# Chunk attention feeding a bilinear feed-forward: values of one unit and scores of the next in one run on the 64x64 tiles

## The chip, the cores and the metric

The kernel runs on one core of one Trainium2 chip. TensorE (PE) does the matrix products, VectorE (DVE), ScalarE (ACT) and GpSimd (POOL) the elementwise work, and SyncE (SP) issues the transfers. The metric is the device time of one execution in microseconds (us): 309.52 us is the median of three runs of the kernel before (309.21 to 310.18).

## The reference

Attention is local: a sequence of 576 positions is cut into chunks of 64, and each chunk attends to itself alone. Its result, 4608 tokens by 512 features, goes through a bilinear feed-forward layer.

```python
B, H, S, D = 8, 8, 576, 64           # chunks of 64 along S
scores = q_c @ k_c.T / sqrt(D)       # 64x64 for each chunk and head
attn = exp(scores - max)
attn = attn / (sum(attn) + 1e-9)
x = (attn @ v_c) as (B*S, H*D)       # 4608 x 512
out = ((x @ w_a) * (x @ w_b)) @ w_out  # d_ff = 1536
```

All inputs and the output are float32; the kernel computes in bfloat16 and float16 with float32 sums.

## The kernel before

**Tiling.** The 4608 tokens are nine blocks K of 512 tokens, each of two units U of 256. A unit's attention is four steps: `scores(U)` (L244) makes 32 matmuls of 64x64 and two Exp activations on ACT (L260); `sums(U)` (L262) makes four matmuls of 64x512 with ones and two Ln activations (L277); `inverse(U)` is one Exp on ACT (L286); `values(U)` (L290) makes 32 matmuls of 64x64 and two multiplications on DVE that leave `xT` in float16 (L309). The 64x64 matmuls use the array as four quarter tiles; all others use the whole 128x128.

**The feed-forward layer.** From block 2 on, both layers are computed by a seven-product (Strassen-like) scheme on 2x2 blocks. A `Group(K, i)` (L394, i = 0 to 5, 256 columns of the inner dimension) makes the seven products p1 to p7 of the first layer, each of four matmuls of 128x256 (L412). Its sums live in three PSUM banks: A (`pa`), B (one of two `pb` banks in turn) and C (`pc`). ACT copies between products: A into B after p1 (L430), and u, b, v out to SBUF after p6, p2, p5 (L423). `add7` adds v and u on DVE (L450, L451; L451 rewrites C), and after p3 and p4 DVE multiplies B and C into `ab` (L462, twice). p3 and p4 of a group come in the next group's time. `OutGroup(K)` (L498) makes the second layer of the block before in 14 parts (n, th), n = 0 to 6, each of six matmuls (L548). n = 0 and 1 go to A (bank `po`), n = 2, 3 and 5 to B (bank `pq`), n = 4 and 6 to C (`po` again). After (0, 1) ACT copies A into B (L560), after (1, 1) A out (L563), after (2, 1) B out as `uo_sb` (L568), after (3, 1) B out as `vo_sb` (L571), after (5, 1) B out (L575).

**Order.** The order on each engine is the order in which the program issues the work (`manual_schedule`). A group's time has two halves. Written as (i, half) of block K:

| | PE order in half 0 | PE order in half 1 |
|---|---|---|
| group i | p1; parts; p3 of the group before; attention; p6; p4 of the group before | p2; parts; attention; p5; p7 |

How many parts of the second layer are issued in each half is in `chunks` (L802); what attention step is issued is in `attention` (L776 to L799), where U = 2K + 2, the first unit of the next block. In blocks 3 and later: sums U at (0, 0), inverse U at (1, 0), values U at (1, 1), scores U+1 at (2, 1), sums U+1 at (3, 0), inverse at (3, 1), values U+1 at (4, 1), `combine_x` for the next block at (5, 0) (two DVE additions, L392), scores U+2 at (5, 1). Block 2 issues scores U itself at (0, 0) and sums U at (0, 1). There is no attention work left in block 8.

**Banks and loads.** PSUM has eight banks: `pa`, `pc`, `po`, `pq` one each, `pb` and `pt` two each. From the end of block 1 every attention step takes its two banks from `pt` (`spread`, L767). Loads, casts (POOL, L207) and DMA transposes (SP, L234) of a unit are issued by `bring` at (1, 0) and (3, 0), some groups ahead of their use.

Of the kernel before, what the change touches and what calls it, by code (L numbers as in the profile page):

```python
# [16 lines left out]
def kernel(  # L17
# [14 lines left out]
    PSUM = bass.MemoryType.PSUM  # L32
# [9 lines left out]
    NKT = DM // 128  # L42
# [3 lines left out]
    NBLK = NTOK // BLK  # L46
    NU = NTOK // UNIT
    WCOL = 256
    NWP = DFF // WCOL
# [12 lines left out]
    c_pool = ctx.enter_context(tc.tile_pool(name="csb", bufs=1))  # L62
    o_pool = ctx.enter_context(tc.tile_pool(name="osb", bufs=2))
    psum_a = ctx.enter_context(tc.tile_pool(name="psuma", bufs=1, space=PSUM))
    psum_b = ctx.enter_context(tc.tile_pool(name="psumb", bufs=2, space=PSUM))
    psum_c = ctx.enter_context(tc.tile_pool(name="psumc", bufs=1, space=PSUM))
    psum_o = ctx.enter_context(tc.tile_pool(name="psumo", bufs=1, space=PSUM))
    psum_q = ctx.enter_context(tc.tile_pool(name="psumq", bufs=1, space=PSUM))
# [10 lines left out]

    spread = [psum_t, psum_b, psum_a, psum_c, psum_t, psum_b, psum_o, psum_q]  # L80
    bank_names = {
        id(psum_a): "pa", id(psum_b): "pb", id(psum_c): "pc",
        id(psum_o): "po", id(psum_q): "pq", id(psum_t): "pt",
    }

    def bank(pool=None):
        if pool is None:
            pool = spread[0]
            spread.append(spread.pop(0))
        return pool.tile([128, 512], FP32, name=bank_names[id(pool)])  # L90

    def keep_warm(n):

        t = bank()
        for _ in range(n):
            nc.tensor.matmul(t, warm_in[:, :128], warm_in, start=True, stop=True)
# [115 lines left out]
    def transpose_pe(U, names="qk"):  # L212
        if U not in qkt:
            qkt[U] = qkt_pool.tile([128, 2, 2, NKT, 128], BF16, name="qkt")
        for n in names:
            w = "qk".index(n)
            src = raw.pop((n, U))
            tp = bank().bitcast(BF16).rearrange("c (i m p) -> c i m p", i=2, m=NKT)
            for i in range(2):
                for m in range(NKT):  # L220
                    nc.tensor.transpose(
                        tp[:, i, m, :],
                        src[:, i, 2 * m:2 * m + 2, :].rearrange("p j d -> p (j d)"),
                        identity,
                    )
            dst = qkt[U][:, w].rearrange("c g m (p i) -> c i m g p", i=2)
            for i in range(2):
                cp = nc.vector.tensor_copy if w == 0 or U == 1 else nc.scalar.copy
                cp(out=dst[:, i], in_=tp[:, i].rearrange("c m (g p) -> c m g p", g=2))
# [11 lines left out]
    ln_of = {}  # L241
    rs_of = {}

    def scores(U):  # L244
        t = qkt.pop(U)
        E_of[U] = sm_pool.tile([128, 2, NKT, 2, 64], BF16, name="E")
        sc = [bank().rearrange("p (m g s) -> p m g s", m=NKT, g=2) for _ in range(2)]
        for m in range(NKT):
            for g in range(2):
                for j in range(2):  # L250
                    for cl in range(2):
                        nc.tensor.matmul(  # L252
                            sc[j][cl * 64:cl * 64 + 64, m, g, :],
                            t[j * 64:j * 64 + 64, 1, g, m, cl * 64:cl * 64 + 64],
                            t[j * 64:j * 64 + 64, 0, g, m, cl * 64:cl * 64 + 64],
                            start=True,
                            stop=True,
                        )
        for j in range(2):
            nc.scalar.activation(out=E_of[U][:, j], in_=sc[j], func=AF.Exp, scale=scale)  # L260
# [55 lines left out]
    def slot(s=None, f=None):  # L316

        if s is not None and s >= NU:
            s = None
        if f is not None:  # L320
            sums(f)
            inverse(f)
        if s is not None:
            scores(s)
        if f is not None:
            values(f)
# [51 lines left out]
    def combine_x(K, parts=(0, 1, 2, 3)):  # L378
        xT = x_tiles[K]
        x11, x12 = xT[:, 0:2, 0:256], xT[:, 2:4, 0:256]  # L380
        x21, x22 = xT[:, 0:2, 256:512], xT[:, 2:4, 256:512]
        if K not in s_of:
            s_of[K] = [s_pool.tile([128, 2, 256], FP16, name=f"s{j}") for j in range(1, 5)]
        s1, s2, s3, s4 = s_of[K]
        for part in parts:
            o, x0, x1, op = (
                (s1, x21, x22, ADD),
                (s2, s1, x11, SUB),
                (s3, x11, x21, SUB),
                (s4, x12, s2, SUB),  # L390
            )[part]
            nc.vector.tensor_tensor(out=o, in0=x0, in1=x1, op=op)  # L392
# [233 lines left out]
    with tc.manual_schedule(  # L626
# [24 lines left out]
        cast_ab(3)  # L651
        transpose_pe(1, "q")
        scores(0)
        transpose_pe(1, "k")
        sums(0, halves=None)
        keep_warm(2)
        scores(1)
        inverse(0)
        values(0)
# [114 lines left out]
        assert not halves and not combos  # L774

        attention = {}  # L776
        for K in range(2, NBLK):
            U = 2 * K + 2
            for at, f, u in (
                ((0, 0) if K == 2 else (-1, 1), scores, U),  # L780
                ((0, 1) if K == 2 else (0, 0), sums, U),
                ((1, 0), inverse, U),
                ((1, 1), values, U),
                ((2, 1), scores, U + 1),
                ((3, 0), sums, U + 1),
                ((3, 1), inverse, U + 1),
                ((4, 1), values, U + 1),
                ((5, 0), lambda u: combine_x(u // 2, (0, 1)), U + 1),
            ):
                if u < NU:  # L790
                    at = (K - 1, NWP - 1, 1) if at[0] < 0 else (K, *at)
                    attention[at] = [lambda f=f, u=u: f(u)]

        for K in range(2, NBLK):
            attention.setdefault((K, 0, 0), []).insert(0, lambda K=K: combine_x(K, (2, 3)))

        def attend(K, i, n):
            for f in attention.get((K, i, n), ()):
# [2 lines left out]
        last = None  # L801
        chunks = {  # L802
            2: (0, 1, 1, 1, 1, 1, 2, 2, 1, 1, 2, 1),
            4: (1, 1, 1, 1, 1, 1, 2, 2, 1, 1, 1, 1),
            NBLK - 1: (1,) * 12,
        }

# [7 lines left out]
        for K in range(2, NBLK):  # L815
            for i in range(NWP):
# [14 lines left out]
                if i == 0:  # L831
                    g = OutGroup(K - 1)
# [72 lines left out]
```

## Time and profile before

| | |
|---|---|
| median of three runs | 309.52 us (309.21 to 310.18) |
| the profiled execution: own time, span | 309.52 us, 307.7 us |
| PE busy | 293.1 us (95%) |
| DVE, ACT, POOL busy | 207.9, 196.1, 192.8 us |
| granted TensorE clock | 1.000 |
| blocks 3 to 6, each | 30.40 us, PE busy 30.40 us |
| 64x64 matmuls | 576 of scores (L252), 576 of values (L300) |

The profile lists each instruction with its start and its duration. A row "x4" is four instructions of one line merged: its duration runs from the first start to the last end. Matmuls are pipelined, so a row's duration is longer than the time to the next row; what a group of matmuls costs is read from start to start. What stands in brackets at a row's end is the idle time of its engine just before it, and who ended it. 1.8 us of the execution's time lie outside the span.

### The profile page before, as it was taken

How to read it: one execution, taken by the hardware profiler on the slowest of the kernel's cores; microseconds unless marked ns; L12 is line 12 of the kernel's file. 1: busy time of each engine (PE TensorE's matmuls, PEld its weight loads, DVE VectorE, ACT ScalarE, POOL GpSimd, SP SyncE). 2: the span in 40 equal slices, each digit the busy share in tenths (PEclk: the TensorE clock that was granted, in tenths of full speed). 3: DMA queues.
4: the chain of work that ended last, by engine and by line, in shares of the span. 5: the costliest groups of instructions: out<-in, count | busy, mean ns of one | idle time of the engine just before them, and what ended most of it. 6: DMA issues, size and time to landing. Idle time of an engine off the chain costs nothing.

```text
span 307.7 us, 8535 instructions
## 1 busy us (share of the span) xinstructions
PE 293.1 (95%) x3499; PEld 231.4 (75%) x3499; DVE 207.9 (68%) x339; ACT 196.1 (64%) x353; POOL 192.8 (63%) x180
## 2 busy tenths in 40 slices
PE   2879999999999999999999999999999999999995
PEld 1534467766577888888888888888888888888884
DVE  3445863996755587678766876687668757965772
ACT  1653567348486678676867686758676877567532
POOL 0565658994899678817873776377647701680560
PEclk9999999999999999999999999999999999999999
DMA  7999999999999998399639934993593000300025
GB/s 228 314 372 288 263 321 356 230 226 213 237 202 246 238 212 238 74 203 216 197 86 232 277 94 103 226 287 77 116 158 138 2 0 2 138 0 4 0 84 191
DMA packets 143079, 54.56 MB, mean 177 GB/s; under 512 B 120256, under 2 KB 137152, under 8 KB 143040
## 3 DMA queue, kind: packets, MB, share of 16 engines
q1 hardware_dynamic: 142896, 53.88, 70.3%
q8 instruction: 27, 0.44, 0.6%
q10 hardware_dynamic: 144, 0.13, 0.1%
q14 instruction: 12, 0.10, 0.1%
HBM read 37.75 MB, written 9.44 MB: 153 GB/s over the span
## 4 chain that ended last, share of the span: by engine, by line
PE 81%; DMA 7%; DVE 4%; ACT 3%; issue 2%; POOL 1%; SPq 1%; ACTq 0%; DVEq 0%; POOLq 0%
PE pb L412 18%; PE pc L412 12%; PE po L548 12%; PE pa L412 11%; PE pq L548 9%; PE pb L616 3%; DMA st<-in_moe_w_b_dram 3%; DMA st<-in_k_dram 2%; DMA st<-in_q_dram 2%; PE po L362 2%; PE pt L267 2%; PE pt L252 2%; PE pc L362 2%; PE pt L300 2%; PE pq L362 2%
## 5 line engine op out<-in xcount | busy, mean ns | idle before, releaser
L492 POOL TENSOR_TENSOR so<-ab_sb 128x512 f16<-128x512 f16 x23 | 26.6, 1155 | 47.1 <-DVE ab_sb L462 47.1
L412 PEld LDWEIGHTS <-t 128*128 128x128 f16 x504 | 48.3, 98 | 9.8 <-issue 3.6
L450 DVE TENSOR_TENSOR c_sb<-pc,v_sb 128x512 f32<-128x512 f32 x42 | 28.9, 687 | 37.8 <-ACT v_sb L423 37.1
L412 PE MATMUL pb<-s,wa 128*128 128x256 f16 x336 | 50.7, 273 | 0.0
L412 PE MATMUL pa<-xT,wb 128*128 128x256 f16 x336 | 50.4, 273 | 0.0
L548 PEld LDWEIGHTS <-ab_sb 128*128 128x128 f16 x384 | 37.6, 98 | 4.7 <-issue 0.4
L423 ACT COPY u_sb<-pb 128x512 f32<-128x512 f32 x42 | 24.7, 588 | 23.5 <-PE pb L412 23.3
L412 PEld LDWEIGHTS <-wb 128*128 128x128 f16 x336 | 32.9, 98 | 4.0
L412 PEld LDWEIGHTS <-wa 128*128 128x128 f16 x336 | 30.9, 98 | 4.4 <-issue 0.2
L462 DVE SCALAR_TENSOR_TENSOR ab_sb<-pc,c_sb 128x512 f16<-128x512 f32 x42 | 28.9, 689 | 6.8 <-PE pc L412 5.4
L207 POOL CAST k_raw<-st 128x1024 bf16<-128x1024 f32 x17 | 18.4, 1081 | 22.3 <-DMA st<-in_k_dram 22.3
L548 PEld LDWEIGHTS <-so 128*128 128x128 f16 x288 | 28.0, 98 | 4.3 <-ACT uo_sb L568 1.0
L462 DVE SCALAR_TENSOR_TENSOR ab_sb<-pb,b_sb 128x512 f16<-128x512 f32 x42 | 28.9, 688 | 3.0 <-PE pb L412 2.6
L423 ACT COPY b_sb<-pa 128x512 f32<-128x512 f32 x42 | 25.0, 595 | 8.5 <-PE pa L412 7.3
L430 ACT COPY pb<-pa 128x512 f32<-128x512 f32 x42 | 24.6, 585 | 8.0 <-PE pa L412 8.0
L207 POOL CAST v_raw<-st 128x1024 bf16<-128x1024 f32 x18 | 19.3, 1073 | 16.1 <-DMA st<-in_v_dram 12.7
L451 DVE TENSOR_TENSOR pc<-pc,u_sb 128x512 f32<-128x512 f32 x42 | 29.0, 690 | 0.0
L423 ACT COPY v_sb<-pb 128x512 f32<-128x512 f32 x42 | 24.8, 591 | 6.1 <-PE pb L412 6.0
L492 POOL TENSOR_TENSOR so<-so,ab_sb 128x512 f16<-128x512 f16 x23 | 26.7, 1160 | 1.8
L492 POOL TENSOR_TENSOR ab_sb<-ab_sb 128x512 f16<-128x512 f16 x23 | 26.6, 1157 | 0.0
L309 DVE TENSOR_TENSOR xT<-pt,ln 128x512 f16<-128x512 f32 x30 | 19.4, 685 | 10.2 <-PE pt L300 10.2
L492 POOL TENSOR_TENSOR so<-ab_sb,so 128x512 f16<-128x512 f16 x23 | 26.1, 1166 | 0.0
(128 smaller groups left out, 577.7 us busy)
## 6 DMA issues: line engine op xcount, KB each, us to landing
out_dram<-o_sb SPq DMA_DIRECT2D x34, 256.0 KB, 3.6
st<-in_v_dram SPq DMA_DIRECT2D x32, 256.0 KB, 4.3
st<-in_q_dram SPq DMA_DIRECT2D x25, 256.0 KB, 5.0
st<-in_k_dram SPq DMA_DIRECT2D x25, 256.0 KB, 3.5
st<-in_moe_w_b_dram SPq DMA_DIRECT2D x6, 512.0 KB, 7.5
st<-in_moe_w_a_dram SPq DMA_DIRECT2D x6, 512.0 KB, 7.4
st<-in_moe_w_out_dram SPq DMA_DIRECT2D x6, 512.0 KB, 6.7
st<-in_q_dram SPq DMA_DIRECT2D x3, 512.0 KB, 5.8
```

The source lines that it names most:

```text
L207: eng.tensor_copy(out=raw[n, U], in_=staged.pop((n, U)))
L309: nc.vector.tensor_tensor(out=x.rearrange("p m (g c s) -> p m g c s", g=2, c=2)[:, :, :, cl, :], in0=av[cl], in1=rs[:, cl].rearrange("p m ...
L362: nc.tensor.matmul(ps[n], w_ab[n, i][:, kt, o:o + 128], xT[:, kt, c0:c1], start=(kt == 0), stop=(kt == NKT - 1),)
L412: nc.tensor.matmul(t[:, h * 256:h * 256 + 256], w[:, kt, h * 128:h * 128 + 128], x[:, kt], start=start and h == 0 and kt == 0, stop=h == 1 ...
L423: nc.scalar.copy(out=t, in_=src)
L430: nc.scalar.copy(out=self.B, in_=self.A)
L450: nc.vector.tensor_tensor(out=self.c, in0=self.C, in1=self.v, op=ADD)
L451: nc.vector.tensor_tensor(out=self.C, in0=self.C, in1=self.u, op=ADD)
L462: nc.vector.scalar_tensor_tensor(out=self.dst[:, :, c0:c0 + 256], in0=t.rearrange("p (h n) -> p h n", h=2), scalar=AB_SCALE, in1=o.rearran ...
L492: (eng or nc.gpsimd).tensor_tensor(out=o, in0=x0, in1=x1, op=op)
L548: nc.tensor.matmul(t[:, c0:c0 + 256], a[:, kt, th * 128:th * 128 + 128], w[:, kt], start=n in (0, 4) and first and kt == 0, stop=last and ...
L616: nc.tensor.matmul(out_ps[K, tg], ab_tiles[K][:, ft, tg * 128:tg * 128 + 128], wo_sb[:, ft], start=(ft == 0), stop=(ft == NFT - 1),)
```

## The change

In blocks 2 to 7, `values(U)` moves from (1, 1) to (2, 1), just ahead of `scores(U+1)`, which stays there. In blocks 3 to 6, `scores(U+2)` moves from (5, 1) to (4, 1), just behind `values(U+1)`. These scores no longer use the `pt` banks: one half goes to a bank of the second layer (`po` at (2, 1), `pq` at (4, 1)), the other to the `pb` bank that the group before has left (`psum_b[0]`). For that the two `pb` banks become two pools that are taken in turn. Among the scores' matmuls only the first on each quarter tile has `start` set. In `chunks`, blocks 3 to 7 issue their parts in another rhythm; the total stays 14.

```diff
-    psum_b = ctx.enter_context(tc.tile_pool(name="psumb", bufs=2, space=PSUM))
+    psum_b0 = ctx.enter_context(tc.tile_pool(name="psumb0", bufs=1, space=PSUM))
+    psum_b1 = ctx.enter_context(tc.tile_pool(name="psumb1", bufs=1, space=PSUM))
+    psum_b = [psum_b0, psum_b1]
...
+        if pool is psum_b:
+            pool = psum_b[0]
+            psum_b.append(psum_b.pop(0))
         return pool.tile([128, 512], FP32, name=bank_names[id(pool)])
...
-    def scores(U):
+    def scores(U, pools=(None, None)):
...
-        sc = [bank().rearrange("p (m g s) -> p m g s", m=NKT, g=2) for _ in range(2)]
+        sc = [bank(p).rearrange("p (m g s) -> p m g s", m=NKT, g=2) for p in pools]
...
-                            start=True,
+                            start=m == 0 and g == 0,
                             stop=True,
+                            skip_group_check=True,
...
+        def at(K, i, n, f, u):
+            if u < NU:
+                attention.setdefault((K, i, n), []).append(lambda: f(u))
+
+        def scores_beside(pool):
+            return lambda u: scores(u, (pool, psum_b[0]))
+
         for K in range(2, NBLK):
...
+            U = 2 * K + 2
+            if K == 2:
+                at(K, 0, 0, lambda u: combine_x(2, (2, 3)), U)
+                at(K, 0, 0, scores, U)
+                at(K, 0, 1, sums, U)
+            else:
+                attention[K, 0, 0] = [lambda K=K: combine_x(K, (2, 3))]
+                at(K, 0, 0, sums, U)
+            at(K, 1, 0, inverse, U)
+            at(K, 2, 1, values, U)
+            at(K, 2, 1, scores_beside(psum_o), U + 1)
+            at(K, 3, 0, sums, U + 1)
+            at(K, 3, 1, inverse, U + 1)
+            at(K, 4, 1, values, U + 1)
+            if K == 2:
+                at(K, 5, 1, scores, U + 2)
+            else:
+                at(K, 4, 1, scores_beside(psum_q), U + 2)
+            at(K, 5, 0, lambda u: combine_x(u // 2, (0, 1)), U + 1)
...
-            4: (1, 1, 1, 1, 1, 1, 2, 2, 1, 1, 1, 1),
+            4: (1, 1, 1, 1, 1, 2, 1, 2, 2, 0, 1, 1),
```

Counted in parts, blocks 3 to 7 issue (2, 1) and (3, 0) together in half (2, 1), where before (2, 1) stood there alone and (3, 0) and (3, 1) together in (3, 0); and (5, 0) and (5, 1) together in (4, 0), where before (5, 1) stood in (4, 1).

More of the change, by code (lines that the diff above doesn't have):

```diff
@@ L81 @@
     bank_names = {
-        id(psum_a): "pa", id(psum_b): "pb", id(psum_c): "pc",
+        id(psum_a): "pa", id(psum_b0): "pb0", id(psum_b1): "pb1", id(psum_c): "pc",
         id(psum_o): "po", id(psum_q): "pq", id(psum_t): "pt",
@@ L776 @@
         attention = {}
+        def at(K, i, n, f, u):
[3 more added lines that the diff above has]
+            return lambda u: scores(u, (pool, psum_b[0]))
         for K in range(2, NBLK):
             U = 2 * K + 2
[L779 to L795, printed above, removed]
+            if K == 2:
[16 more added lines that the diff above has]
+            at(K, 5, 0, lambda u: combine_x(u // 2, (0, 1)), U + 1)
         def attend(K, i, n):
```

## The prediction

> **What bounds the kernel now.** I read the page's busy table, then each block as one window, then the chain that ended last, then the timeline around each attention step, with PE, ACT and DVE side by side.
>
> ```profile
> PE 293.1 (95%) x3499; PEld 231.4 (75%) x3499; DVE 207.9 (68%) x339; ACT 196.1 (64%) x353; POOL 192.8 (63%) x180
> PE 81%; DMA 7%; DVE 4%; ACT 3%; issue 2%; POOL 1%; SPq 1%; ACTq 0%; DVEq 0%; POOLq 0%
> 143.70:174.10 30.40, 30.40 (x412) 25.71 (x396) 21.90 (x37) 22.24 (x39) 19.65 (x18) 1.00 0.81 186
> ```
>
> PE is 95% of the span and 81% of the chain that ended last. The third line is one block (143.70 to 174.10), with its length and then PE, PEld, DVE, ACT and POOL busy and the clock: PE busy 30.40 of 30.40 us at the full granted clock, DVE 21.90, ACT 22.24, POOL 19.65. In blocks 3 to 7 PE is the bound without a visible hole; whatever shortens PE's stream there shortens the run, and whatever makes PE wait lengthens it. A run of 64x64 matmuls looks like this (timeline, PE):
>
> ```profile
> 137.83 0.82 PE L548 MATMUL pq<-wo,so 128*128 128x256 f16 x6
> 138.58 0.45 PE L300 MATMUL pt<-E,v_raw 64*64 64x64 bf16 x32
> 138.96 0.61 PE L412 MATMUL pb<-s,wa 128*128 128x256 f16 x4
> 139.40 0.60 PE L412 MATMUL pc<-s,t 128*128 128x256 f16 x4
> ```
>
> 128x256 matmuls start 0.109 us apart (twelve take 1.31, from 129.21 to 130.52), so six take 0.656 and four 0.437. From 137.83 to 139.40 are 1.57 us; less 0.656 and 0.437, the run of 32 costs 0.48. Its row lasts 0.45, and one matmul lasts 0.19 (median 193 ns), so its first and last start are 0.26 apart. The other 0.22 are the passage in and out.
>
> **Part 1, ten runs joined (gain).** Values and scores become neighbours six times at (2, 1) (blocks 2 to 7) and four times at (4, 1) (blocks 3 to 6). Each saves one passage, 0.22: 10 x 0.22 = 2.2 us. That two kinds of 64x64 matmul can abut is seen in the only place where they do already, in the start-up at a slower pace: scores rows every 0.05 up to 13.54, the first values row at 13.60. Bounds: the scores' first matmuls carry waits (on the bank's earlier users, on the transposes) that now stand inside the run. If they break it in two, p5, p7 and with them ACT's v_sb are all later, and the saving is 0; more than 2.2 is excluded, since nothing else of the matmuls goes away. I take 2.2, because all that is waited for is old by then: block 3's transposes for (4, 1) are issued at 126.53 and 127.91, eleven us ahead of 138.58; the resting `pb` bank was last read by the first L462, which starts 0.6 after p3 (p3 135.99, L462 136.81) and ends over 1 us before the scores.
>
> **Part 2, the second layer's rhythm (loss).** In blocks 3 to 7 parts (2, 1) and (3, 0) now stand back to back in half (2, 1). (2, 1) finishes B in `pq`; ACT copies it out (L568); (3, 0) adds to the same bank and must wait for that copy. Before, p5, p7 and p1 and a run of scores lay between. Block 2 has this pair back to back already, and its rows carry the forecast (timeline):
>
> ```profile
> 97.04 0.82 PE L548 MATMUL pq<-wot,so 128*128 128x256 f16 x6
> 97.90 0.59 ACT L568 COPY uo_sb<-pq 128x512 f32<-128x512 f32 x1
> 98.54 0.83 PE L548 MATMUL pq<-wo,so 128*128 128x256 f16 x6 [0.68 <-ACT uo_sb L568]
> ```
>
> 97.04 to 98.54 is 1.50 where 0.656 would do: PE loses 0.84. The copy started 0.04 after the last product ended, so the loss is bare latency (end of product, 0.59 of copy, 0.05 back). In the changed blocks ACT is free too: b_sb (L423) starts 0.64 after p2 and the part ends 0.44 + 0.82 = 1.26 after it. Behind the waiting part stand values and scores on PE, and nothing overtakes. 5 x 0.84 = 4.2 us. Bounds: 3.9 if the next work finds its operands a little earlier, 4.4 if ACT is late by one semaphore. Against this pair speaks also the Trainium skill, "Perfetto Trace Analysis", Matmuls: independent groups should rotate through different PSUM banks so that an evacuation overlaps the next group. By that rule in reverse, a same-bank pair pays its whole evacuation, which is what block 2's row shows; the sum keeps the row.
>
> **Part 3, p4 after the joined run (loss).** The two Exps stand on ACT ahead of v_sb, v_sb ahead of add7 on DVE, and p4 on PE waits for L451. Scores at (5, 1) show the delays:
>
> ```profile
> 143.43 0.44 PE L252 MATMUL pt<-qkt 64*64 64x64 bf16 x32
> 143.92 1.09 ACT L260 ACTIVATE E<-pt 128x512 bf16<-128x512 f32 x2 [0.45 <-PE pt L252]
> 144.89 0.59 ACT L423 COPY v_sb<-pb 128x512 f32<-128x512 f32 x1
> 145.51 0.69 DVE L450 TENSOR_TENSOR c_sb<-pc,v_sb 128x512 f32<-128x512 f32 x1 [0.86 <-ACT v_sb L423]
> 146.12 0.69 DVE L451 TENSOR_TENSOR pc<-pc,u_sb 128x512 f32<-128x512 f32 x1
> ```
>
> Exps 0.49 after the run's start, v_sb 0.97 later, L450 0.62, L451 0.61, end 0.69. In a joined run starting at T the scores start 0.26 later, so L451 ends at T + 3.64 and p4 may start at T + 3.69 (136.22 + 0.69 to the p4 at 136.96 is 0.05). DVE's two L309 are over by then: 139.07 to 140.36 is T + 0.49 to T + 1.78. PE's own path: run 0.64 (0.38 + 0.26), p5, p7, p1 at 0.44 each with 0.01 of start-up, one part 0.656, p3 0.44, p6 0.44: p4 is due at T + 3.49 in (5, 0), where no sums stand in between. It waits 0.2, in four blocks: 0.8 us. At (3, 0) the sums add 0.44 (146.31 to 146.65 and 0.1 of entry), p4 is due at T + 3.93 and waits for nothing, although only one part is left as cover there. After a late p4, its L462 stands on DVE behind L451 (T + 2.95), the L462 of p3 (0.61 later) and two L392 (171.98 to 173.38 is 1.40 from L462 to L462): start T + 4.96, end T + 5.65. p7 writes the same bank and is due two products, a part and p5 after p4, at T + 5.66; I take 0.05 each, 0.2 us. Bounds: 0 and 0.5 per block for both.
>
> The Trainium skill's "TensorEngine Tiling (Array Packing)", PSUM Bottleneck, speaks against joining at all: tiling speeds up the products and not their evacuation, which may become the bottleneck. If that held everywhere, the 2.2 of part 1 would be gone and the sum 4.7 instead of 2.5; by the rows it holds at (4, 1) and not at (2, 1).
>
> **Part 4, a stall that goes.** p4 at (4, 0) waits for L451 today:
>
> ```profile
> 136.22 0.69 DVE L451 TENSOR_TENSOR pc<-pc,u_sb 128x512 f32<-128x512 f32 x1
> 136.43 0.60 PE L412 MATMUL pb<-s,t 128*128 128x256 f16 x4
> 136.96 0.60 PE L412 MATMUL pc<-xT,t 128*128 128x256 f16 x4
> ```
>
> p6 to p4 takes 0.53, not 0.44. A second part in (4, 0) covers it: -0.09 in blocks 3 to 7, -0.5 us.
>
> **At nothing.** (a) Values later by a group: `xT` is next read by combine_x at (5, 0), after the later unit in any case; the v cast that reuses its buffer runs at 138.20 in block 3 and 165.69 in block 4, (2, 1) is at 127.5 and 157.9. The sums at (3, 0) now need L309 done: T + 1.78 against T + 3.1. (b) Scores U+2 earlier: `pq` is copied out (L575) over 1 us earlier, since (5, 1) is now issued in (4, 0). (c) SP's and POOL's lists keep their order; two stores go out half a group earlier. (d) The start flag and the split pool change no count of instructions.
>
> **Sum.** -2.2 + 4.2 + 0.8 + 0.2 - 0.5 = +2.5. The profiled execution took 309.52, which is also the median: **312.0 us**.
>
> **Rivals.**
> - *Faster.* The wait of part 2 doesn't reach PE: -2.2 + 0.8 + 0.2 - 0.5 = -1.7, 307.8. For it: ACT has 8 us free in each block, so the copy is never queued; against it, in block 2 it was not queued either, and PE waited. The sign turns where the pair costs below (2.2 + 0.5 - 1.0) / 5 = 0.34 a block; 0.59 of copy alone is more. Chance 0.05.
> - *The change doesn't do what it says*: the joined run breaks at the scores' waits, no passage is saved: 309.5 + 4.7 = 314.2. Chance 0.08.
> - *ACT and DVE become the bound around the joined runs*: p4 late at (3, 0) as well (margin 0.24 in five blocks) and p7 by the full 0.5: 2.5 + about 1.5, 313.5. For it: the margins above are a quarter of a microsecond; against: ACT and DVE have 8 us free per block. Chance 0.10.
> - *A near balance*, part 2 half covered and parts 3 nil: -2.2 + 2.1 - 0.5, about 309. Chance 0.05.
> - *The forecast*: 0.72, own range 311.0 to 313.2.
>
> **How the numbers follow.** A difference under 0.3% (0.9 us) can't be told from none. Slower: 0.72 + 0.08 + 0.10 = 0.90; same 0.05; faster 0.05. The range leaves out the fast cases and the far end of the broken run: 310.7 to 313.8.
>
> **What the profile after would show.** Part 1: rows L300 and L252 adjoining, the next L412 about 0.64 after the first L300. Part 2: five holes of 0.84 before an L548 into `pq`, released by ACT `uo_sb` L568, just ahead of each run at (2, 1). Part 3: p4 (L412 into `pc`) released by DVE L451 at (5, 0) in four blocks. Part 4: no hole at (4, 0). The forecast is wrong if those five holes are not there or are much shorter, or if the run is broken in its middle.

## The result, and the profile after

The changed kernel takes 313.06 us in the median of four runs (312.62 to 313.27), the kernel before 309.70 us in four (309.21 to 310.18). The ratio is 1.0107 with a 95% interval of 1.0086 to 1.0127: slower by about 1.1%. The profiled execution took 312.62 us against 309.52, its span is 310.8 us against 307.7. The forecast was 312.0 us with a range of 310.7 to 313.8, and slower with a chance of 0.90.

Line numbers of the changed kernel are larger by 5 at the scores' matmuls (L257, L252 before) and by 6 behind them: L554 is the second layer's product (L548 before), L574 the copy of `uo_sb` (L568), L418 the first layer's products (L412), L306 the values (L300), L457 the second half of add7 (L451).

The page of the changed kernel: busy time, the chain by engine, and the group of products into B of the second layer, with the idle time ahead of it; the last line is the same group before.

```profile
PE 292.6 (94%) x3499; PEld 231.9 (75%) x3499; DVE 212.1 (68%) x339; ACT 195.7 (63%) x353; POOL 192.7 (62%) x180
PE 79%; ACT 8%; DVE 7%; issue 2%; DMA 2%; POOL 0%; SPq 0%; ACTq 0%; DVEq 0%
L554 PE MATMUL pq<-wo,so 128*128 128x256 f16 x180 | 23.7, 272 | 4.0 <-ACT uo_sb L574 4.0
L548 PE MATMUL pq<-wo,so 128*128 128x256 f16 x180 | 23.7, 273 | 0.7 <-ACT uo_sb L568 0.7
```

PE's share of the chain falls from 81% to 79%, ACT's rises from 3% to 8%. The idle time ahead of the products into `pq` is 4.0 us, where the same group had 0.7 before: block 2's hole of then, and five new ones. One window of the changed kernel, from one joined run at (2, 1) to the next (its length, then PE, PEld, DVE, ACT and POOL busy, clock, DMA):

```profile
159.37:190.41 31.04, 30.29 (x389) 25.78 (x388) 22.21 (x35) 22.20 (x39) 19.64 (x19) 1.00 0.74 171
```

This window is 31.04 us long, where one block's window before was 30.40, and PE now stands idle for 0.75 of them. The timeline at (2, 1), PE and ACT, shows both halves of the forecast, the hole and the joined run (of the 32 scores two merged rows stand here; in this timeline and those below some rows between the ones shown are left out):

```profile
157.14 0.82 PE L554 MATMUL pq<-wot,so 128*128 128x256 f16 x6
157.99 0.59 ACT L574 COPY uo_sb<-pq 128x512 f32<-128x512 f32 x1
158.63 0.81 PE L554 MATMUL pq<-wo,so 128*128 128x256 f16 x6 [0.67 <-ACT uo_sb L574]
159.38 0.44 PE L306 MATMUL pt<-E,v_raw 64*64 64x64 bf16 x32
159.65 0.20 PE L257 MATMUL po<-qkt 64*64 64x64 bf16 x2
159.66 0.20 PE L257 MATMUL pb<-qkt 64*64 64x64 bf16 x2
...
160.04 0.61 PE L418 MATMUL pb<-s,wa 128*128 128x256 f16 x4
160.49 0.60 PE L418 MATMUL pc<-s,t 128*128 128x256 f16 x4
```

157.14 to 158.63 is 1.49 us for six matmuls that need 0.656; the idle part is 0.84 by the start times to the nanosecond. The first scores start 0.27 after the first values, without a break. And at (5, 0), PE and DVE:

```profile
203.43 0.69 DVE L456 TENSOR_TENSOR c_sb<-pc,v_sb 128x512 f32<-128x512 f32 x1 [0.62 <-ACT v_sb L429]
203.66 0.60 PE L418 MATMUL pb<-s,wa 128*128 128x256 f16 x4
204.03 0.69 DVE L457 TENSOR_TENSOR pc<-pc,u_sb 128x512 f32<-128x512 f32 x1
204.10 0.60 PE L418 MATMUL pb<-s,t 128*128 128x256 f16 x4
204.78 0.60 PE L418 MATMUL pc<-xT,t 128*128 128x256 f16 x4
```

p4 (204.78) starts 0.68 after p6 instead of 0.44: it waits for L457, which ends at 204.72.

### The profile page after: what moved, and what is told of

The parts are those of the page before. It is cut to its first block, busy times and chain, and to the rows that moved or that the text cites. A ratio compares the mean times of both kernels' runs of the same rounds, so it can differ in the third digit from the quotient of the medians.

```text
span 310.8 us, 8539 instructions
## 1 busy us (share of the span) xinstructions
PE 292.6 (94%) x3499; PEld 231.9 (75%) x3499; DVE 212.1 (68%) x339; ACT 195.7 (63%) x353; POOL 192.7 (62%) x180
## 4 chain that ended last, share of the span: by engine, by line
PE 79%; ACT 8%; DVE 7%; issue 2%; DMA 2%; POOL 0%; SPq 0%; ACTq 0%; DVEq 0%
PE pb L418 16%; PE pc L418 11%; PE pa L418 11%; PE po L554 11%; PE pq L554 9%; PE pb L622 3%; PE pb L368 3%; ACT E L266 2%; PE pc L368 2%; PE po L368 2%; DMA st<-in_q_dram 2%; PE pt L273 2%; PE pt L306 2%; ACT ln L283 2%; ACT uo_sb L574 1%
## 5 line engine op out<-in xcount | busy, mean ns | idle before, releaser
L418 PEld LDWEIGHTS <-t 128*128 128x128 f16 x504 | 48.3, 98 | 10.6 <-issue 4.9
L418 PE MATMUL pb<-s,wa 128*128 128x256 f16 x336 | 50.5, 273 | 0.0
L418 PE MATMUL pa<-xT,wb 128*128 128x256 f16 x336 | 50.4, 273 | 0.0
L554 PEld LDWEIGHTS <-ab_sb 128*128 128x128 f16 x384 | 37.6, 98 | 4.7 <-issue 0.4
L418 PEld LDWEIGHTS <-wb 128*128 128x128 f16 x336 | 32.9, 98 | 4.0
L418 PEld LDWEIGHTS <-wa 128*128 128x128 f16 x336 | 31.7, 98 | 4.2 <-issue 0.2
L554 PEld LDWEIGHTS <-so 128*128 128x128 f16 x288 | 28.0, 98 | 8.5 <-issue 4.2
L457 DVE TENSOR_TENSOR pc<-pc,u_sb 128x512 f32<-128x512 f32 x42 | 29.0, 690 | 0.0
L554 PE MATMUL pq<-wo,so 128*128 128x256 f16 x180 | 23.7, 272 | 4.0 <-ACT uo_sb L574 4.0
```

The costliest lines, as they stand in the source:

```text
L418: nc.tensor.matmul(t[:, h * 256:h * 256 + 256], w[:, kt, h * 128:h * 128 + 128], x[:, kt], start=start and h == 0 and kt == 0, stop=h == 1 ...
L457: nc.vector.tensor_tensor(out=self.C, in0=self.C, in1=self.u, op=ADD)
L554: nc.tensor.matmul(t[:, c0:c0 + 256], a[:, kt, th * 128:th * 128 + 128], w[:, kt], start=n in (0, 4) and first and kt == 0, stop=last and ...
```

## The experiments

Two theories stand against each other. A: the loss is the pair of parts (2, 1) and (3, 0) on one bank, and joining the runs itself gains. B: the joined runs are the loss, since they fill four banks at once that ACT and DVE must empty; any hole that is taken away at one place comes back at the next. A block's length, below, is from one sums run (3, 0) to the next in the profile; it is 30.42 us before and 31.03 to 31.10 after.

**1. The pair apart, joined runs kept.**

```diff
-            4: (1, 1, 1, 1, 1, 2, 1, 2, 2, 0, 1, 1),
+            4: (1, 1, 1, 1, 1, 1, 2, 2, 2, 0, 1, 1),
```

> The changed kernel with parts (2,1) and (3,0) apart again (blocks 3 to 7: 1,1,1,1,1,1,2,2,2,0,1,1); all ten joined runs stay. Theory A (the same-bank pair is the loss, joining itself gains): the five holes of 0.84 us go, ten joins at 0.20 remain, the wait of p4 at (5,0) stays at 0.24 in four blocks: 312.6 - 4.2 = about 308.4 us, faster than before by some 0.3%. Rival B (ACT and DVE are the bound around the joined runs, and the hole would only move): 311 us or more, with p4 at (3,0) or the sums waiting instead.

Measured: ratio to the kernel before 0.9969 (0.9946 to 0.9992), profiled execution 308.63 us, blocks of 30.20 us (30.27 and 30.42 in two, where p4 or p7 waits a little longer for DVE). The five holes are gone and don't come back elsewhere in the blocks. Timeline, PE and ACT, at (2, 1):

```profile
157.08 0.45 PE L306 MATMUL pt<-E,v_raw 64*64 64x64 bf16 x32
157.19 0.59 ACT L574 COPY uo_sb<-pq 128x512 f32<-128x512 f32 x1
157.75 0.61 PE L418 MATMUL pb<-s,wa 128*128 128x256 f16 x4
158.20 0.60 PE L418 MATMUL pc<-s,t 128*128 128x256 f16 x4
158.63 0.60 PE L418 MATMUL pa<-xT,wb 128*128 128x256 f16 x4
159.07 1.47 PE L554 MATMUL pq<-wo,so 128*128 128x256 f16 x12
```

The copy of `uo_sb` now lies beside the joined run, and (3, 0) follows at 159.07, long after its end. A holds, B falls: with all ten joined runs in place the kernel is faster than before.

**2. The rhythm of parts alone, on the kernel before.**

```diff
-            4: (1, 1, 1, 1, 1, 1, 2, 2, 1, 1, 1, 1),
+            4: (1, 1, 1, 1, 1, 2, 1, 2, 2, 0, 1, 1),
```

> The kernel before with the changed rhythm of parts alone (blocks 3 to 7); no run is joined, scores and values stay where they were and in the pt banks. Theory A: five holes of 0.84 us, the wait of p4 at (4,0) gone (-0.5): 309.5 + 3.7 = about 313.2 us, with no wait of p4 at (5,0). Rival B: the rhythm costs little without the joined runs, 309.5 us.

Measured: ratio 1.0143 (1.0100 to 1.0186), profiled execution 314.33 us, blocks of 31.16 us. The loss is there without a single joined run. 31.16 less 30.42 is 0.74; 0.84 for the hole less 0.09 for p4 at (4, 0), which no longer waits, is 0.75. The profiled execution is 1.1 us above the expected time; 0.9 of that had gone by block 2's sums at (3, 0) (100.62 us against 99.73), a stretch that this edit doesn't touch and where p4 (94.3) and a part of the second layer (99.9) start late, by 0.15 and 0.33.

**3. Joined at (2, 1) alone, with the rhythm of the kernel before.**

```diff
-            if K == 2:
-                at(K, 5, 1, scores, U + 2)
-            else:
-                at(K, 4, 1, scores_beside(psum_q), U + 2)
+            at(K, 5, 1, scores, U + 2)
...
-            4: (1, 1, 1, 1, 1, 2, 1, 2, 2, 0, 1, 1),
+            4: (1, 1, 1, 1, 1, 1, 2, 2, 1, 1, 1, 1),
```

> Joined runs at (2,1) alone (six), scores U+2 stay at (5,1) in the pt banks, the rhythm of parts of the kernel before. Theory A: six passages of 0.20 saved and nothing lost: 308.3 us; the wait of p4 at (4,0) (0.09) stays. Rival B: the four banks that fill at once at (2,1) delay p4 or p3 at (3,0); 309.5 us or more.

Measured: ratio 0.9983 (0.9953 to 1.0012), no difference that the times alone can show; profiled execution 308.70 us, blocks of 30.22 to 30.23 from block 4 on (in block 3, 30.44, p7 waits once for DVE). By the profile a joined run saves 0.193 (30.418 less 30.225), and nothing at (3, 0) waits. The experiment also prices the joins at (4, 1): with them and the part that moved (experiment 1) a block is 30.20, without them 30.22. There the saving of 0.19 is more than eaten by the waits behind it (p4 0.24, p7 0.02); what is left of a gain is the 0.09 that the moved part saves at (4, 0).

**4. The Exps behind v_sb at (4, 1).** On top of experiment 1, the two Exps of the scores at (4, 1) are issued later: one behind p5's copy `v_sb`, one behind the copy of A into B of the next group. Only the scores at (4, 1) are given the list `later`.

```diff
...
+        def exp(j):
+            nc.scalar.activation(out=E[:, j], in_=sc[j], func=AF.Exp, scale=scale)
+
+        if later is not None:
+            later += [lambda: exp(1), lambda: exp(0)]
+            return
...
                 now.p1()
+                if later:
+                    later.pop(0)()
...
                 now.p5()
+                if later:
+                    later.pop(0)()
```

> As the run with the pair apart, and at (4,1) of blocks 3 to 6 the two Exps stand behind v_sb on ACT: one directly behind it, the other behind the copy of A into B after the next p1. If the wait of p4 at (5,0) comes from the Exps ahead of v_sb, it goes (0.24 in four blocks) and the time is about 1 us below the run with the pair apart, some 307.4 us. If DVE is what is late there (its two multiplications of the values), nothing changes; if the second Exp only moves the delay to the copy of A into B, p6 at (5,0) waits about as much as p4 did.

Measured: ratio 0.9938 (0.9915 to 0.9961) against 0.9969 (0.9946 to 0.9992) of experiment 1, blocks of 29.95 to 30.07 against 30.20 and more. The two intervals overlap; it is the blocks and the rows that show the gain. Timeline, ACT, DVE and PE (in this kernel L437 is `v_sb`, L268 the Exps, L444 the copy of A into B, L464 and L465 add7, L426 the products):

```profile
171.37 0.58 ACT L437 COPY v_sb<-pb 128x512 f32<-128x512 f32 x1 [0.62 <-PE pb L426]
171.85 0.60 ACT L268 ACTIVATE E<-pb 128x512 bf16<-128x512 f32 x1
171.98 0.69 DVE L464 TENSOR_TENSOR c_sb<-pc,v_sb 128x512 f32<-128x512 f32 x1 [0.15 <-ACT v_sb L437]
172.49 0.57 ACT L444 COPY pb<-pa 128x512 f32<-128x512 f32 x1
172.59 0.69 DVE L465 TENSOR_TENSOR pc<-pc,u_sb 128x512 f32<-128x512 f32 x1
172.97 0.60 ACT L268 ACTIVATE E<-pq 128x512 bf16<-128x512 f32 x1
173.13 0.60 PE L426 MATMUL pb<-s,t 128*128 128x256 f16 x4
173.57 0.60 PE L426 MATMUL pc<-xT,t 128*128 128x256 f16 x4
```

p4 (173.57) follows p6 after 0.44 again, in all four blocks. DVE wasn't what was late: it waited for `v_sb`, and `v_sb` for the Exps. The profiled execution took 309.50 us; in it one part in block 2 waited 2.1 us for POOL's `so`. The median of the ten runs, 308.12 us, is 1.4 lower; whether others had such a wait isn't known, since one was profiled.

**5. A dose: other work between the two parts.** The changed kernel, with p2 between (2, 1) and (3, 0), or with the whole joined run between them.

```diff
-                now.p2()
-                chunk(chunks.get(K, chunks[4])[2 * i + 1])
+                if i == 2 and 2 < K < NBLK - 1:
+                    chunk(1)
+                    now.p2()
+                    chunk(1)
...
```

> The changed kernel, with p2 of the half (2,1) issued between the parts (2,1) and (3,0) instead of ahead of both (blocks 3 to 7). Theory A (PE waits for one copy of the bank between the two parts, 0.84 us of latency): p2's four matmuls are 0.44 us of other work, so each hole shrinks from 0.84 to 0.40: 5 x 0.44 = 2.2 us less than the changed kernel, ratio to the kernel before about 1.004. A rival, that the hole is a fixed cost of a semaphore wait in PE's queue and not the copy's latency: the holes stay at 0.84 and the ratio at 1.011.

```diff
-                chunk(chunks.get(K, chunks[4])[2 * i + 1])
-                attend(K, i, 1)
+                if i == 2 and 2 < K < NBLK - 1:
+                    chunk(1)
+                    attend(K, i, 1)
+                    chunk(1)
...
```

> The changed kernel, with the joined run of values and scores at (2,1) standing between the parts (2,1) and (3,0) (blocks 3 to 7), p5 behind the second part. Theory A: the run and its passages are 0.66 to 0.77 us of other work, so a hole of 0.07 to 0.18 is left of 0.84; ratio about 0.998. Later v_sb gets a part's time of cover, so nothing else should wait; the rest of the waits (p4 at (5,0), 0.24) stays. If holes of 0.84 stay, the copy was not the cause.

Measured: with p2 between, ratio 1.0036 (1.0018 to 1.0054); with the run between, 0.9978 (0.9956 to 0.9999). Timeline, PE and ACT, first p2 between, then the joined run between:

```profile
187.35 0.82 PE L554 MATMUL pq<-wot,so 128*128 128x256 f16 x6
188.01 0.60 PE L418 MATMUL pa<-xT,wb 128*128 128x256 f16 x4
188.21 0.59 ACT L574 COPY uo_sb<-pq 128x512 f32<-128x512 f32 x1 [0.46 <-PE pq L554]
188.84 0.81 PE L554 MATMUL pq<-wo,so 128*128 128x256 f16 x6 [0.24 <-ACT uo_sb L574]
```

```profile
187.27 0.45 PE L306 MATMUL pt<-E,v_raw 64*64 64x64 bf16 x32
187.37 0.59 ACT L574 COPY uo_sb<-pq 128x512 f32<-128x512 f32 x1
188.01 0.81 PE L554 MATMUL pq<-wo,so 128*128 128x256 f16 x6
```

From the start of p2 to the part after it are 0.83 us where 0.44 would do: a hole of 0.40. From the joined run to the part are 0.74 where a run that p5 follows takes 0.66: 0.08. So the hole is 0.84 less the other work in between, as the latency of one copy would have it: 0 gives 0.84, 0.44 gives 0.40, 0.75 (the run, 0.66, and its way in, 0.09) gives 0.08. A fixed cost of the wait in PE's queue is excluded. Beside this, p4 at (5, 0) waits up to 0.09 longer than in the changed kernel in three blocks with p2 between and in one with the run between; the cause is open.

**6. The start flags alone, on the kernel before.**

```diff
-                            start=True,
+                            start=m == 0 and g == 0,
                             stop=True,
+                            skip_group_check=True,
```

> The kernel before with the changed start flags of the scores' matmuls alone. All theories: nothing; the 32 matmuls of scores take 0.38 us from their start to the next product as before, 309.5 us, ratio 1.000.

Measured: ratio 1.0016 (0.9992 to 1.0039), blocks of 30.42 us, as before. No cost shows.

**7. All that helped, together.** Experiment 4, with block 7 in the rhythm of the kernel before and block 2's pair apart.

```diff
-            2: (0, 1, 1, 1, 1, 1, 2, 2, 1, 1, 2, 1),
+            2: (0, 1, 1, 1, 1, 2, 1, 2, 1, 1, 2, 1),
             4: (1, 1, 1, 1, 1, 1, 2, 2, 2, 0, 1, 1),
+            7: (1, 1, 1, 1, 1, 1, 2, 2, 1, 1, 1, 1),
```

> Everything that helped, together: ten joined runs, the pair apart in blocks 3 to 6, the Exps at (4,1) behind v_sb, block 7 with the rhythm of the kernel before, and in block 2 the pair (2,1), (3,0) apart too (0,1,1,1,1,2,1,2,1,1,2,1). Theory A: against the run with the Exps behind v_sb (ratio 0.994) block 2's hole of 0.84 and block 7's 0.2 go: ratio about 0.990, some 306.6 us. If block 2 is held up by its transfers instead, its hole goes and the same time is lost a little later: ratio 0.993.

Measured: ratio 0.9934 (0.9905 to 0.9963), median 307.17 us against 309.76 of the kernel before in the same session, profiled execution 306.77 us. It beats both kernels. That block 2's and block 7's edits add to experiment 4 is seen in the profile alone: p7 in block 7 is on time, and from the first p6 of block 2 (83.63 us, 83.82 in experiment 1) to its sums at (3, 0) are 14.85 us against 15.70 in experiment 1, so the hole of 0.84 isn't lost again there. By the times experiment 4 and this one can't be told apart, and the expected 0.990 lies just outside the interval. What makes single runs of these kernels differ by 2 us and more (306.1 to 309.9 here) was not settled; in the profiles the stretch that differs most is block 2 and what comes before it.

## Why the prediction was right

**Direction and bound.** Right: blocks 3 to 7 were PE's alone, and what PE waits for there adds to the time one for one. A block grew by 31.03 - 30.42 = 0.61 us; the terms as measured give -0.39 + 0.84 + 0.24 + 0.02 - 0.09 = 0.62.

**Part 1, joined runs.** Right in kind: nine of the ten run through without a break, and the one at (4, 1) of block 3 pauses for 0.06 us ahead of its last scores (the cause is open). The size was a little too good. Six matmuls started at 158.63, so the seventh was due at 159.29; the passage in takes 0.09, the run 0.66 to p5 (0.64 was forecast) and 0.01 at p5: 0.77 for a joined run against 0.96 for two lone ones, a saving of 0.19 instead of 0.22; ten times that, less the pause, is 1.9 instead of 2.2. One reading of rows was off: by those named (135.99, 136.81) the first L462 starts 0.82 after p3 and not 0.6. It ends over 1 us before the scores all the same, so nothing hung on it.

**Part 2, the pair on one bank.** Right, in place and size: five holes of 0.84, released by the copy of `uo_sb`, 4.2 us. It was the only reason why the change lost: experiment 1 takes it away and is faster, experiment 2 has it alone and is slower. The rule on rotating banks from the Trainium skill ("Perfetto Trace Analysis", Matmuls) that was set against the pair speaks of independent groups, and these two aren't: (3, 0) adds to the sum that (2, 1) leaves in the bank, so it can't go to another bank without a copy more. What the rule is for, other products running beside the copy, is what experiment 1 restores and experiment 2 lacks.

**Part 3, p4 at (5, 0).** Right, 0.24 instead of 0.20 in four blocks; p7 behind it waited 0.02 instead of 0.05. At (3, 0) nothing waits, as forecast. The rule from "TensorEngine Tiling (Array Packing)", PSUM Bottleneck, points to the right place, since the joins at (4, 1) gain nothing by themselves (experiments 1 and 3: 30.20 against 30.22 a block, with 0.09 of part 4 in the first). But experiment 4 shows that it was the order on ACT and not its or DVE's capacity: with the Exps behind `v_sb` the same evacuations fit.

**Part 4.** Right: p4 at (4, 0) starts on time in the changed kernel, 0.09 in each of five blocks.

**What was left out.** In block 7 no scores follow at (4, 1), but the part that stood there is gone all the same. POOL's three additions that the multiplication after p4 of (4, 0) releases so lie a part later against PE, and the third now runs beside DVE's addition for the next block at (5, 0). POOL, DVE and PE there, first before, then after:

```profile
262.38 1.16 POOL L492 TENSOR_TENSOR ab_sb<-ab_sb 128x512 f16<-128x512 f16 x1
263.84 0.41 DVE L392 TENSOR_TENSOR s<-xT 128x512 f16<-128x512 f16 x1
265.00 0.60 PE L412 MATMUL pb<-s,wa 128*128 128x256 f16 x4
265.44 0.60 PE L412 MATMUL pc<-s,t 128*128 128x256 f16 x4
```

```profile
265.88 1.15 POOL L498 TENSOR_TENSOR ab_sb<-ab_sb 128x512 f16<-128x512 f16 x1
266.68 0.63 DVE L398 TENSOR_TENSOR s<-xT 128x512 f16<-128x512 f16 x1
267.84 0.60 PE L418 MATMUL pb<-s,wa 128*128 128x256 f16 x4
268.43 0.60 PE L418 MATMUL pc<-s,t 128*128 128x256 f16 x4
```

The addition takes 0.63 us instead of 0.41, the multiplication of C behind it is later by as much, and p7 at (5, 1) starts 0.59 after p5 instead of 0.44: 0.15 us of waiting that the sum didn't have. In block 8's first group p7 waits 0.07 longer than before, and there too the addition ahead of it takes 0.07 longer (1.03 us, 0.97 before). Both are read from the rows; no run tries the overlap by itself. With these 0.2 and the sizes above (+0.3 from part 1, +0.05 from part 3) the sum is 3.1; the profiled executions differ by 3.1. The remaining 0.4 up to the median lies within the scatter of the runs (the profiled one is the lowest of the four), and no trace shows where it goes.

**Rivals.** The fast case is out: it needed a pair that costs PE under 0.34 us a block, and the pair cost 0.84. The broken run didn't occur, the pause of 0.06 aside. ACT and DVE as the bound occurred only at (5, 0), with the price that the forecast gave it; the near balance needed half of the hole covered, and none of it was.

## What to carry to other kernels

When the order of work on a saturated engine is reshuffled, look at what has become neighbours: two pieces of work on one buffer with a copy in between cost the copy's whole latency back to back (0.84 us here) and nothing with that much other work between them. A gain from joining small runs is real but small (0.2 us a join), and one misplaced neighbour in each block outweighs several of them. Before an engine is called too slow for a burst of evacuations, look at the order of its queue: the one copy that the critical product needs should stand first.

## What was not expected of the hardware

DVE's additions in float16 (`combine_x`, L398 in the changed kernel) take 0.41 to 0.43 us when POOL is idle. In the blocks from 3 on, one that starts while a POOL addition is running ends about 0.28 us after that one's end, where that is later than it would end alone: it took 0.59 us where POOL had 0.31 to go (before, 147.32), 0.82 where it had 0.54 (before, 142.18), 1.04 where it had 0.76 (below). Where POOL had 0.06 to go (experiment 7, 171.44), it took 0.42. That can move p7. In the profile of experiment 7, DVE, POOL and PE in block 3:

```profile
140.54 1.15 POOL L506 TENSOR_TENSOR ab_sb<-ab_sb 128x512 f16<-128x512 f16 x1
140.94 1.04 DVE L406 TENSOR_TENSOR s<-xT 128x512 f16<-128x512 f16 x1
142.01 0.42 DVE L406 TENSOR_TENSOR s<-s,xT 128x512 f16<-128x512 f16 x1
142.35 0.69 DVE L476 SCALAR_TENSOR_TENSOR ab_sb<-pc,c_sb 128x512 f16<-128x512 f32 x1
143.09 0.60 PE L426 MATMUL pc<-s,t 128*128 128x256 f16 x4 [0.40 <-DVE ab_sb L476]
```

The first addition overlaps POOL's from 140.94 to 141.69 and takes 1.04, the second takes 0.42; the multiplication after them is later by some 0.6, and p7 (143.09) loses 0.57 us (0.68 from the matmul before, where 0.11 would do). In this execution p7 lost time so in block 3 only; in blocks 4 to 6 POOL's addition had 0.06 to go at that place, in block 7 none ran. The single waits of p7 in experiment 1 (block 5) and experiment 3 (block 3) also stand behind a slow addition, of 0.64 and 1.18 us. That the overlap is the cause was seen in the rows and not tried by itself.
